# Float64 weights split ahead of their units and parked in DRAM

## The chip, the cores and the metric

One core of one Trainium2 chip runs the kernel. The metric is device time in microseconds (us) of one execution. Five engines work side by side, each through its own instructions in the order in which they were written: TensorE (PE), VectorE (DVE), ScalarE (ACT), GpSimd (POOL), and SyncE (SP), which issues nearly all DMAs.

## The reference

```python
# attention: state = w*state + k v^T per head, y = r (state + u k v^T)
x = attn_out.transpose(0, 2, 1, 3).reshape(B * S, H * D)       # 1536 x 384, float32
# layer 1: four experts of width 1024
p = domain_probs / (domain_probs.sum(-1, keepdims=True) + 1e-09)
for e in range(4):
    h = np.maximum(x @ w1[e], 0.0)
    out += p[:, e:e + 1] * (h @ w2[e])
# layer 2: width 2048, elu
h = x @ w_in
g = np.where(h > 0.0, h, alpha * (np.exp(np.minimum(h, 0.0)) - 1.0))
return (g @ w_out).astype(np.float32)
```

`w_in` and `w_out` of layer 2 are float64 arrays; all other inputs are float32.

## The kernel before

The attention runs in chunks of 128 tokens. Both layers run as six **units** of 1024 hidden columns: units 0 to 3 are the four experts, units 4 and 5 the two halves of the second layer. A unit goes over the 1536 tokens in blocks of 512 (unit 0, beside the attention, in blocks of 256), and a block has eight **steps** f = 0 to 7 of 128 hidden columns. A step issues a first-layer product `st1` (9 matmuls, line 610, into a bank `ph`), evacuates it (`evac`), and then issues the second-layer product `st2` (9 matmuls, line 646, into the three banks `po0` to `po2`) of an earlier step: two steps back in units 0 to 3, three steps back in units 4 and 5.

Every product is made of float32r parts: a weight `wh` (high) and `wl` (low), and an activation `hh` and `hl`. In units 0 to 3 ACT writes `hh` (line 622) and DVE `hl` (line 623). In units 4 and 5 `evac` is a longer chain: ACT writes `m` twice (lines 629, 630), DVE `g` (632), ACT `hh` (634), POOL `hl` (635). At the end of a block `po` is emptied: in units 1 to 3 by DVE into `t` (666), which POOL adds to `acc` (667), and after unit 3 ACT and POOL write from `acc` the new input of layer 2, `xh` (672) and `xl` (673); in unit 4 ACT copies `po` to `acc` (684).

A unit's weights are eight **slices** of 128 x 768 values: four of the first product, `(u, 1, i)`, and four of the second, `(u, 2, i)`. `split` (lines 493 to 538) turns a slice into `wh` and `wl` in one of 14 slots in SBUF (8, and NX = 6 once the attention's room is free). A float32 slice takes one copy on ACT and one subtraction on DVE. A float64 slice is read as two 32-bit words and takes eight DVE instructions (lines 519 to 534), a copy on ACT (529) and an addition on POOL (535), in four **stages** of two DVE instructions, with a yield behind each. `work` (540) is called behind every step but f = 1 and 2 and runs stages until its budget is spent; a stage "costs" 1.3 to 1.7, the budget is 0.9 up to unit 2 and 1.6 from unit 3 on:

```python
                    if not u or not BA <= f <= BB:
                        self.work(0.9 if u < NE - 1 else 1.6)
```

A slot is given back by `done` when the last block's product that reads it has been issued; the next `split` takes it. Slices are loaded by SP into three `raw` buffers (lines 482, 484). The order on every engine is that of the Python calls; nothing reorders it later.

Of the kernel before, what the change touches and what calls it, by code (L numbers as in the profile page):

```python
# [22 lines left out]
P = 128  # L23
B, H, S, D = 2, 8, 768, 48
NP = H // 2          # head pairs; a pair sits on partitions 0-47 and 64-111
NCB = S // P         # 128-token chunks of a batch row
NCH = B * NCB
N = B * S            # tokens
DM = H * D
KD = DM // P  # L30
NE, FF = 4, 1024     # experts, their width
NU = NE + 2          # the second layer's 2048 columns count as two more units
NF = FF // P
NX = 6               # slots for weights in the attention's room
WARM = 12            # products of zeros ahead of the first
NS = (2, 1, 2, 1, 1, 1, 1, 1)    # the attention's steps by step of the layers' first block
BA, BB = 1, 2        # the steps of a block that no weights are split in
TB = 512             # tokens of a block
# [8 lines left out]
# the upper words of float64s, read as float32s: of the largest and the least normal float32  # L47
# [3 lines left out]
class Fast:  # L51
    """Attention in chunks of 128 tokens, decays as w^t and w^-(s+1), which
    needs W_LO <= w <= W_HI (elsewhere w is held there, and the general path is taken).

    Rows of a pair of heads: 64 j + (index in the head). The chunk's part of a head's output,
    with its index on the rows, is v^T A + S^T r, where A[s, t] is (k_s w^-(s+1)).(r_t w^t)
    for s < t and r.u.k for s = t."""
# [27 lines left out]
    def bank(self):  # L85
        """The next bank: of three, and of the two layers' while those wait for the first x."""
        pool, tag = self.banks[self.nbank % len(self.banks)]
        self.nbank += 1
        return pool.tile([P, 512], F32, tag=tag, name=tag)

    def warm(self, n):
        """Products of zeros: the array's clock is halved while it has little to do."""
        nc = self.g.nc
        if self.zero is None:
            self.zero = self.c.tile([P, 512], BF16, name="zero")
            nc.vector.memset(self.zero, 0.0)
        pz = self.g.php.tile([P, 512], F32, tag="ph1", name="ph1")
        for _ in range(n):
            nc.tensor.matmul(pz, self.zero[:, 0:P], self.zero, start=True, stop=True)

    # r, k with their index on the rows
# [9 lines left out]
    # r, k, or v, with the tokens on the rows  # L111
# [49 lines left out]
    def setup_masks(self):  # L161
        nc = self.g.nc
        # 1 where t > s
        mf = self.c.tile([P, P], F32, name="mf")
        nc.gpsimd.memset(mf, 0.0)
        nc.gpsimd.affine_select(
            out=mf, in_=mf, compare_op=ALU.is_ge, fill=1.0, base=0,
            pattern=[[-1, P]], channel_multiplier=1)
        nc.gpsimd.tensor_copy(self.mask, mf)
# [25 lines left out]
    # r or k, scaled  # L195
# [9 lines left out]
    # the keys decayed to the chunk's end  # L205
# [6 lines left out]
    # r.u.k, by entries  # L212
# [8 lines left out]
    # the diagonal  # L221
    def s1d(self, ci):
# [3 lines left out]
        if ci < 2:  # L226
            # the first chunks' diagonal goes by itself
            self.va[ci] = va = self.p2.tile([P, DM], F32, tag="va", name="va")
            nc.vector.tensor_tensor(
                out=va.rearrange("t (h d) -> t h d", h=H), in0=self.v[ci].rearrange("t (h d) -> t h d", h=H),  # L230
                in1=a0.rearrange("s (h o) -> s h o", o=1).to_broadcast([P, H, D]), op=ALU.mult)
            return
# [10 lines left out]
    def s2(self, ci):  # L243
        nc = self.g.nc
        st = self.st[ci]
        # a bank for each of the two places of a head in its pair
# [13 lines left out]
    # the state's change, and the state  # L260
    def s3u(self, ci):
# [5 lines left out]
        # side by side, a head of a pair in each half of the array's columns  # L267
# [30 lines left out]
    def s3(self, ci):  # L298
# [5 lines left out]
        for p in range(NP):  # L304
# [4 lines left out]
            for j in range(2):  # L309
                # at first, all rows up to the second head's are to be written  # L310
                h, m = 2 * p + j, D if c or j else 64
                nc.tensor.matmul(  # L312
                    py[64 * j:64 * j + m, p, :], v[:, h * D:h * D + m], A[:, j, p, :],
                    start=not c, stop=True)
# [5 lines left out]
        if o:  # L320
            # the rows of all heads together, by way of DRAM
# [8 lines left out]
    # the first chunks': the rows of all heads together at once, v and S between zeros  # L330
# [5 lines left out]
    def s3f(self, ci):  # L336
# [3 lines left out]
        for kk in range(KD):  # L340
            # side by side, 64 rows of x in each half of the array's columns
# [22 lines left out]
class General:  # L364
    """Attention for any w: each state entry's recurrence is scanned along the tokens, with
    the key's index on the partitions and one column of the state at a time."""
# [8 lines left out]
    def run(self, ident, xT):  # L375
# [5 lines left out]
        # sel[:, e]: from row e, 64 + e to the rows of their halves; one: from the rows of a  # L381
        # half, with the window that starts at 64 - e, to row e, 64 + e
# [69 lines left out]
class Gen:  # L452
# [22 lines left out]
    def load_next(self):  # L475
        if self.nraw < len(self.slices):
            s = self.slices[self.nraw]
            u, kind, i = s
            t = self.wp.tile([P, 1536], I32, tag="raw", name="raw", bufs=self.NRAW)
            if u < NE:  # L480
                t = t[:, 0:768].bitcast(F32)
                self.nc.sync.dma_start(out=t, in_=self.ws[u, i, kind - 1])
            else:
                self.nc.sync.dma_start(out=t, in_=self.ws2[u - NE, i, kind - 1])
            self.raw[s] = t
            self.nraw += 1

# [5 lines left out]
    def split(self):  # L493
        """The next slice's two parts, in steps; each yields the time it takes of DVE."""
# [4 lines left out]
        pool, k = self.free.pop(0)  # L499
        self.slot[s] = (pool, k)  # L500
        hi = pool.tile([P, 768], F32R, tag=f"wh{k}", name=f"wh{k}")
        lo = pool.tile([P, 768], F32R, tag=f"wl{k}", name=f"wl{k}")
        if s[0] < NE:
            nc.scalar.copy(hi, t)  # L504
            self.weng.tensor_tensor(out=lo, in0=t, in1=hi.bitcast(F32), op=ALU.subtract)  # L505
            self.load_next()
            self.w_s[s] = (self.shape(hi, s[1]), self.shape(lo, s[1]))
            yield 0.9
            return
        # a float64 as two words: a = sign, exponent and the upper 20 fraction bits as a  # L510
        # float32 (0 below its normal range, its largest above), c = the 32 bits below
# [6 lines left out]
        v = nc.vector  # L518
        v.tensor_scalar(out=hf, in0=hf, scalar1=F64_MAX, scalar2=-F64_MAX, op0=ALU.min, op1=ALU.max)  # L519
# [16 lines left out]
        self.load_next()  # L536
        self.w_s[s] = (self.shape(hi, s[1]), self.shape(lo, s[1]))
        yield 1.7

    def work(self, budget):  # L540
        """Splits ahead, as far as there are slots, for about so much time of DVE."""
        while budget > 0:
            if self.cur is None:
                if not self.free or self.nspl == len(self.slices):
                    return
                self.cur = self.split()
# [20 lines left out]
    def probs(self, dp):  # L567
# [7 lines left out]
        # by expert, then tokens  # L575
# [41 lines left out]
    def evac(self, u, n, ph):  # L617
# [8 lines left out]
        else:  # L626
# [4 lines left out]
            # exp(min(h, 0)) - 1 is 0 where h > 0, and at least h elsewhere  # L631
# [57 lines left out]
    def count(self, c):  # L689
        """How many of w's entries the fast attention holds for."""  # L690
# [13 lines left out]
    def setup(self, ctx):  # L704
# [11 lines left out]
        self.free, self.slot, self.cur, self.weng = [], {}, None, self.nc.vector  # L716
        self.add_slots(self.wp, 8)
        # slices in the order of their splits: (unit, layer, slice)
        self.slices = [(u, kind, i) for u in range(NU) for i in range(4) for kind in (1, 2)]
        self.ident = self.cp.tile([P, P], F32, name="ident")  # L720

    def setup2(self, ctx):
        """What the attention's room is for once it is over."""
# [7 lines left out]
        self.sp = ctx.enter_context(tc.tile_pool(name="sp", bufs=1))  # L731

    def layers(self, tb0, before):
        """Both layers, the first unit in blocks of tb0 tokens. before(u, t0, f) is called
        ahead of a step and gives what is to come after its first product, if anything."""
        pend = []
        for u in range(NU):
            n = TB if u else tb0
            for t0 in range(0, N, n):
                for f in range(NF):  # L740
# [3 lines left out]
                    # the end of a block frees its banks before anything else  # L744
# [8 lines left out]
                    if not u or not BA <= f <= BB:  # L753
                        self.work(0.9 if u < NE - 1 else 1.6)
# [5 lines left out]
    def fast(self):  # L760
        tc, nc = self.tc, self.nc
        with ExitStack() as ctx:
# [21 lines left out]
            # attention; the first two chunks before the layers start  # L784
# [30 lines left out]
            self.work(0.1)   # w1, slice 0  # L815
# [7 lines left out]
            self.work(0.1)   # w2, slice 0  # L823
# [24 lines left out]
            for i in range(2, NCH):  # L848
                steps += [(f, c) for f, c in ((a1, i), (a2, i + 1), (a3, i)) if c < NCH]
                if i % 2 == 0 and i > 2:  # L850
                    # two steps after the last a3 of a pair
# [62 lines left out]
def laid_out(r, k, v, w, u, moe_domain_probs, moe_w1, moe_w2, moe2_w_in, moe2_w_out):  # L914
    def heads(a):       # head entries to rows 64 j + d of the pairs, 0 between
# [5 lines left out]
    # by chunk: rows 64 j + d, then r or k, pair, token; and rows of tokens, then r, k, v, entry  # L921
# [11 lines left out]
    # slices of 256 hidden columns: unit, slice, layer, row, then 768 values  # L933
# [31 lines left out]
```

## Time and profile before

| | |
|---|---|
| runs (3) | median 686.3 us, 685.81 to 689.27 |
| profiled execution, its span | 685.3 us; no other time of that execution is given, the median lies 1.0 us above it |
| TensorE busy | 666.9 us, 97% of the span |
| DVE, ACT, POOL busy | 352.6, 211.5, 208.0 us |
| mean granted TensorE clock | 0.984 |
| DMA | 48.11 MB, mean 70 GB/s |

A profile row is read as "line, engine, operation, out<-in". A name such as `wh` or `po` stands for all tiles of that name, and line numbers are those of the kernel before. "Idle before" is the time in which the engine stood still ahead of an instruction, with what released it. The clock is a share of 2.4 GHz: 1.00 is that level and 0.50 is 1.2 GHz.

### The profile page before, as it was taken

To read this page: it belongs to the slowest core of one execution; us is meant where nothing else is said; L and a number is where in the kernel's file an instruction comes from. 1 tells how busy PE (TensorE), PEld (TensorE's weight loads), DVE (VectorE), ACT (ScalarE), POOL (GpSimd) and SP (SyncE) were. 2 spreads that over 40 slices of the span, in tenths; PEclk is the share of its full clock that TensorE was granted. 3 is DMA by queue.
4 is the path that set the end of the run, shared out by engine and by line. 5 is a ranking of instruction groups with operands and counts; after the bars stand their busy time and mean duration, and the time that the engine had idled before them with its cause. 6 is when DMAs were issued, how large, how long until landed. Compare 5 with 4: busy or idle time off the path is not lost.

```text
span 685.3 us, 9098 instructions
## 1 busy us (share of the span) xinstructions
PE 666.9 (97%) x3701; PEld 557.4 (81%) x3701; DVE 352.6 (51%) x505; ACT 211.5 (31%) x358; POOL 208.0 (30%) x163
## 2 busy tenths in 40 slices
PE   8999999999999999999999999999997999999996
PEld 5788988899888888888888887888875888888884
DVE  7896566324544133422135696569596848212121
ACT  3232221123332113211122123133535454644441
POOL 5564563210002020202021225243744534333331
PEclk7899999999999999999999999999998999999999
DMA  8775542102421003210010221202121100001011
GB/s 256 216 215 165 171 148 69 34 15 70 162 92 47 0 3 107 99 47 0 1 55 38 93 92 47 92 7 88 46 92 46 47 0 1 0 1 47 0 47 52
DMA packets 18661, 48.11 MB, mean 70 GB/s; under 512 B 2145, under 2 KB 7698, under 8 KB 18610
## 3 DMA queue, kind: packets, MB, share of 16 engines
q1 hardware_dynamic: 18464, 47.42, 21.4%
q8 instruction: 31, 0.51, 0.3%
q14 instruction: 20, 0.16, 0.1%
q10 hardware_dynamic: 146, 0.03, 0.0%
HBM read 43.09 MB, written 4.35 MB: 69 GB/s over the span
## 4 chain that ended last, share of the span: by engine, by line
PE 84%; DVE 9%; issue 3%; POOL 2%; ACT 1%; DMA 0%; DVEq 0%; POOLq 0%; ACTq 0%
PE po L646 38%; PE ph L610 37%; PE pa L251 2%; PE pa L306 2%; PE pa L312 2%; DVE raw L519 1%; POOL acc L667 1%; DVE q L530 1%; DVE a L523 1%; DVE g L632 1%; DVE q L520 1%; DVE a L534 1%; DVE hl L623 1%; DVE a L527 1%; POOL wl L535 1%
## 5 line engine op out<-in xcount | busy, mean ns | idle before, releaser
L646 PE MATMUL po<-hh,wh 128*128 128x512 f32 (+1 forms) x504 | 183.4, 364 | 4.9 <-ACT acc L684 4.6
L646 PE MATMUL po<-hl,wh 128*128 128x512 f32 (+1 forms) x504 | 181.9, 361 | 1.9 <-POOL hl L635 1.7
L646 PE MATMUL po<-hh,wl 128*128 128x512 f32 (+1 forms) x504 | 181.5, 360 | 0.0
L610 PE MATMUL ph<-xh,wh 128*128 128x512 f32 (+1 forms) x504 | 177.7, 361 | 0.1
L610 PE MATMUL ph<-xh,wl 128*128 128x512 f32 (+1 forms) x504 | 177.1, 360 | 0.0
L623 DVE SCALAR_TENSOR_TENSOR hl<-ph,hh 128x512 fp32r<-128x512 f32 (+1 forms) x120 | 69.6, 582 | 179.9 <-ACT hh L622 179.2
L622 ACT ACTIVATE hh<-ph 128x512 fp32r<-128x512 f32 (+1 forms) x120 | 61.2, 512 | 281.9 <-PE ph L610 281.9
L610 PE MATMUL ph<-xl,wh 128*128 128x512 f32 (+1 forms) x504 | 126.1, 359 | 0.0
L646 PEld LDWEIGHTS po<-hh,wh 128*128 128x128 f32 x504 | 95.4, 189 | 22.4 <-ACT acc L684 5.0
L646 PEld LDWEIGHTS po<-hl,wh 128*128 128x128 f32 x504 | 95.6, 190 | 17.7 <-POOL hl L635 2.9
L610 PEld LDWEIGHTS ph<-xh,wh 128*128 128x128 f32 x504 | 95.5, 190 | 14.9 <-issue 0.4
L610 PEld LDWEIGHTS ph<-xh,wl 128*128 128x128 f32 x504 | 95.5, 189 | 14.1
L646 PEld LDWEIGHTS po<-hh,wl 128*128 128x128 f32 x504 | 95.5, 190 | 14.0
L610 PEld LDWEIGHTS ph<-xl,wh 128*128 128x128 f32 x504 | 88.3, 189 | 14.1
L635 POOL TENSOR_TENSOR hl<-g,hh 128x512 fp32r<-128x512 f32 x48 | 63.8, 1329 | 100.2 <-ACT hh L634 92.0
L667 POOL TENSOR_TENSOR acc<-acc,t 128x512 f32<-128x512 f32 x27 | 34.1, 1293 | 195.4 <-DVE t L666 195.4
L632 DVE SCALAR_TENSOR_TENSOR g<-m,ph 128x512 f32<-128x512 f32 x48 | 32.9, 684 | 92.0 <-ACT m L630 87.8
L535 POOL TENSOR_TENSOR wl<-a,raw 128x768 fp32r<-128x768 f32 x16 | 29.9, 1868 | 99.2 <-DVE a L534 59.2
L634 ACT CAST hh<-g 128x512 fp32r<-128x512 f32 x48 | 29.8, 622 | 68.0 <-DVE g L632 68.0
L629 ACT ACTIVATE m<-ph 128x512 f32<-128x512 f32 x48 | 28.6, 596 | 28.4 <-PE ph L610 28.2
L505 DVE TENSOR_TENSOR wl<-raw,wh 128x768 fp32r<-128x768 f32 x32 | 33.0, 1032 | 2.3 <-ACT wh L504 1.7
L233 POOL TENSOR_TENSOR A<-ident,a 128x1024 f32<-128x1024 f32 x10 | 20.7, 2071 | 43.5 <-DVE a L225 25.2
(103 smaller groups left out, 513.1 us busy)
## 6 DMA issues: line engine op xcount, KB each, us to landing
raw<-in_ws_dram SPq DMA_DIRECT2D x32, 384.0 KB, 3.0
raw<-in_ws_dram SPq DMA_DIRECT2D x16, 768.0 KB, 4.1
rk<-in_rkv_dram SPq DMA_DIRECT2D x12, 384.0 KB, 5.6
rkT<-in_rkT_dram SPq DMA_DIRECT2D x10, 448.0 KB, 5.2
pb<-pd SPq DMA_DIRECT2D x4, 768.0 KB, 3.9
v<-in_rkv_dram SPq DMA_DIRECT2D x12, 192.0 KB, 6.2
out_dram<-acc SPq DMA_DIRECT2D x9, 256.0 KB, 2.1
xd<-yT SPq DMA_DIRECT2D x10, 192.0 KB, 2.7
```

What stands on the lines that cost most here:

```text
L233: nc.gpsimd.tensor_tensor(out=self.A[ci % 2].rearrange("s j p t -> s p j t"), in0=self.g.ident.rearrange("s (a b t) -> s a b t", a=1, b=1) ...
L505: self.weng.tensor_tensor(out=lo, in0=t, in1=hi.bitcast(F32), op=ALU.subtract)
L535: nc.gpsimd.tensor_tensor(out=lo, in0=af, in1=cf, op=ALU.add)
L610: nc.tensor.matmul(ph[:, 0:n], a[:, kk, c0:c0 + P], b[:, kk], start=q == 0, stop=q == 3 * KD - 1)
L622: nc.scalar.activation(hh[:, 0:n], ph[:, 0:n], AF.Relu)
L623: nc.vector.scalar_tensor_tensor(out=hl[:, 0:n], in0=ph[:, 0:n], scalar=0.0, in1=hh[:, 0:n].bitcast(F32), op0=ALU.max, op1=ALU.subtract)
L629: nc.scalar.activation(m, ph, AF.Relu, scale=-1.0)
L632: nc.vector.scalar_tensor_tensor(out=gg, in0=m, scalar=-1.0, in1=ph, op0=ALU.add, op1=ALU.max)
L634: nc.scalar.copy(hh, gg)
L635: nc.gpsimd.tensor_tensor(out=hl, in0=gg, in1=hh.bitcast(F32), op=ALU.subtract)
L646: nc.tensor.matmul(po[:, 0:n], a[:, ff, i * P:(i + 1) * P], b[:, 0:n], start=f == 0 and q == 0, stop=f == NF - 1 and q == 2)
L667: nc.gpsimd.tensor_tensor(out=a, in0=a, in1=t[:, 0:n], op=ALU.add)
```

## The change

The float64 slices leave `split`. A new generator `narrow` runs the same ten instructions on them from unit 1 on, whenever no float32 slice has a free slot, into one pair of buffers `nh`, `nl`, instead of into a slot. `store` writes the pair to DRAM when the next `narrow` begins; `fetch` loads a stored pair by two DMAs into a slot when one is free and all float32 splits are done. The raw float64 words have two buffers `wide` of their own. NX goes from 6 to 4 (12 slots in all). The budget is 0.9 in unit 0 and 1.2 after.

```diff
-NX = 6               # slots for weights in the attention's room
+NX = 4
...
+    def load_wide(self):
+        if self.nwide < len(self.wide):
+            u, kind, i = self.wide[self.nwide]
+            t = self.sp.tile([P, 1536], I32, tag="wide", name="wide", bufs=2)
+            self.nc.sync.dma_start(out=t, in_=self.ws2[u - NE, i, kind - 1])
+            self.wraw.append(t)
+            self.nwide += 1
...
+    def store(self):
+        if self.made:
+            s, *parts = self.made.pop()
+            self.w_d[s] = d = self.dr.tile([2, P, 768], F32, name=f"w{s[0]}{s[1]}{s[2]}")
+            for i, t in enumerate(parts):
+                self.nc.sync.dma_start(out=d[i], in_=t.bitcast(F32))
+
+    def fetch(self):
+        while self.free and self.nget < len(self.wide) and self.wide[self.nget] in self.w_d:
+            s = self.wide[self.nget]
+            self.nget += 1
+            for i, t in enumerate(self.parts(s)):
+                self.nc.sync.dma_start(out=t.bitcast(F32), in_=self.w_d[s][i])
+
+    def narrow(self):
+        s = self.wide[self.nnar]
+        self.nnar += 1
+        t = self.wraw.pop(0)
+        hi = self.sp.tile([P, 768], F32R, tag="nh", name="nh")
+        lo = self.sp.tile([P, 768], F32R, tag="nl", name="nl")
...
+        self.store()
         v.tensor_scalar(out=hf, in0=hf, scalar1=F64_MAX, scalar2=-F64_MAX, op0=ALU.min, op1=ALU.max)
...
         nc.gpsimd.tensor_tensor(out=lo, in0=af, in1=cf, op=ALU.add)
-        self.load_next()
-        self.w_s[s] = (self.shape(hi, s[1]), self.shape(lo, s[1]))
+        self.made.append((s, hi, lo))
+        self.load_wide()
         yield 1.7
...
             if self.cur is None:
-                if not self.free or self.nspl == len(self.slices):
+                if self.nspl == len(self.slices):
+                    self.fetch()
+                if self.free and self.nspl < len(self.slices):
+                    self.cur = self.split()
+                elif self.sp and self.nnar < len(self.wide):
+                    self.cur = self.narrow()
+                else:
+                    self.store()
                     return
-                self.cur = self.split()
...
-                        self.work(0.9 if u < NE - 1 else 1.6)
+                        self.work(0.9 if not u else 1.2)
```

**DVE at the last steps of unit 3.** Before (`hl` is written once a step; `raw` is a float64 slice, `q` and `a` are scratch):

```order
L623 SCALAR_TENSOR_TENSOR hl_4055<-ph2_4044,hh_4054 128x512
L519 TENSOR_SCALAR raw_3806<-raw_3806 128x768
L520 TENSOR_SCALAR q_4069<-raw_3806 128x768
L523 SCALAR_TENSOR_TENSOR a_4070<-raw_3806,q_4069 128x768
L525 TENSOR_SCALAR q_4069<-raw_3806 128x768
L623 SCALAR_TENSOR_TENSOR hl_4086<-ph3_4075,hh_4085 128x512
L527 SCALAR_TENSOR_TENSOR a_4070<-q_4069,a_4070 128x768
L530 TENSOR_SCALAR q_4069<-a_4070 128x768
L532 SCALAR_TENSOR_TENSOR raw_3806<-raw_3806,q_4069 128x768
L534 TENSOR_TENSOR a_4070<-a_4070,wh11_4067 128x768
```

The same place after the change:

```order
L662 SCALAR_TENSOR_TENSOR hl_4163<-ph2_4152,hh_4162 128x512
L552 TENSOR_SCALAR wide_3973<-wide_3973 128x768
L553 TENSOR_SCALAR q_4197<-wide_3973 128x768
L662 SCALAR_TENSOR_TENSOR hl_4215<-ph3_4204,hh_4214 128x512
L556 SCALAR_TENSOR_TENSOR a_4198<-wide_3973,q_4197 128x768
L558 TENSOR_SCALAR q_4197<-wide_3973 128x768
L662 SCALAR_TENSOR_TENSOR hl_4240<-ph4_4229,hh_4239 128x512
L560 SCALAR_TENSOR_TENSOR a_4198<-q_4197,a_4198 128x768
```

Before, two stages (four instructions) stand between one `hl` and the next; now one stage (two instructions).

**SP over the end of unit 3.** Before, only loads of float64 slices stand there:

```order
L484 DMA raw_3806<-in_ws2_dram 128x1536
L484 DMA raw_3868<-in_ws2_dram 128x1536
L484 DMA raw_4042<-in_ws2_dram 128x1536
L484 DMA raw_4104<-in_ws2_dram 128x1536
L484 DMA raw_4162<-in_ws2_dram 128x1536
```

After (`wh11` and so on are slots, `w412` is the stored pair of slice (4, 1, 2)):

```order
L489 DMA wide_4150<-in_ws2_dram 128x1536
L532 DMA wh11_4175<-w412_3183 128x768
L532 DMA wl11_4176<-w412_3183 128x768
L532 DMA wh2_4179<-w422_3294 128x768
L532 DMA wl2_4180<-w422_3294 128x768
L532 DMA wh1_4183<-w413_3539 128x768
L532 DMA wl1_4184<-w413_3539 128x768
L532 DMA wh3_4187<-w423_3714 128x768
L532 DMA wl3_4188<-w423_3714 128x768
L532 DMA wh4_4191<-w510_3891 128x768
L532 DMA wl4_4192<-w510_3891 128x768
L524 DMA w511_4199<-nh_3998 128x768
```

Ten loads of stored pairs now stand between the load of a float64 slice and the store of the pair (`nh`, `nl`) of slice (5, 1, 1).

**ACT over the change from unit 3 to unit 4.** Before (`hh` of unit 3's last two steps, then unit 4's first `m`):

```order
L622 ACTIVATE hh_4085<-ph3_4075 128x512
L529 CAST wh11_4067<-a_4070 128x768
L622 ACTIVATE hh_4116<-ph4_4106 128x512
L629 ACTIVATE m_4149<-ph0_4137 128x512
L630 ACTIVATE m_4149<-m_4149 128x512
L634 CAST hh_4147<-g_4150 128x512
L529 CAST wh12_4129<-a_4132 128x768
L629 ACTIVATE m_4176<-ph1_4164 128x512
L630 ACTIVATE m_4176<-m_4176 128x512
```

After:

```order
L661 ACTIVATE hh_4214<-ph3_4204 128x512
L661 ACTIVATE hh_4239<-ph4_4229 128x512
L562 CAST nh_4195<-a_4198 128x768
L668 ACTIVATE m_4267<-ph0_4255 128x512
L669 ACTIVATE m_4267<-m_4267 128x512
L673 CAST hh_4265<-g_4268 128x512
L668 ACTIVATE m_4291<-ph1_4279 128x512
L669 ACTIVATE m_4291<-m_4291 128x512
L673 CAST hh_4289<-g_4292 128x512
```

Before, one copy of a slice stands behind unit 4's first `hh` and writes a slot (`wh12`). Now it stands ahead of unit 4's first `m`, and writes `nh`, which the store above reads.

## Rows read from the trace of the kernel before

**Rows 1.** Chain that ended last: shares of the span by engine.

```profile
PE 84%; DVE 9%; issue 3%; POOL 2%; ACT 1%; DMA 0%; DVEq 0%; POOLq 0%; ACTq 0%
```

**Rows 2.** Waits of TensorE: engine, line, releaser: us in total, times, longest.

```profile
PE po L646 <- ACT acc L684: 4.6, 1, 4.6
PE po L646 <- POOL hl L635: 1.7, 2, 1.4
```

**Rows 3.** Timeline, TensorE: start us, us, engine, line, out<-in, [idle before].

```profile
512.15 0.50 PE L646 MATMUL po<-hl,wh 128*128 128x512 f32 x1 [1.40 <-POOL hl L635]
...
520.90 0.80 PE L646 MATMUL po<-hh,wh 128*128 128x512 f32 x1 [4.56 <-ACT acc L684]
...
527.64 0.39 PE L646 MATMUL po<-hh,wh 128*128 128x512 f32 x1
```

**Rows 4.** Windows: us, busy (x) of PE PEld DVE ACT POOL, clock, DMA share, GB/s.

```profile
455.00:470.00 15.00, 15.00 (x68) 12.43 (x67) 14.31 (x17) 3.70 (x6) 3.73 (x2) 1.00 0.16 53
...
512.00:514.00 2.00, 1.85 (x8) 1.53 (x9) 1.86 (x3) 0.00 (x0) 0.10 (x1) 1.00 0.88 349
...
522.00:524.00 2.00, 2.00 (x6) 1.58 (x5) 0.69 (x1) 1.15 (x3) 0.26 (x1) 0.50 0.87 295
```

**Rows 5.** Chain that ended last, in order of time: start us, us, what.

```profile
531.89 2.04 PE po L646 x9
...
670.61 6.81 PE po L646 x30
```

**Rows 6.** Timeline, the change from unit 3 to unit 4.

```profile
468.70 0.39 PE L610 MATMUL ph<-xh,wh 128*128 128x512 f32 x1
...
477.94 1.88 DVE L666 TENSOR_TENSOR t<-po,pb 128x512 f32<-128x512 f32 x3
...
480.58 3.79 POOL L667 TENSOR_TENSOR acc<-acc,t 128x512 f32<-128x512 f32 x3
...
488.09 1.28 POOL L635 TENSOR_TENSOR hl<-g,hh 128x512 fp32r<-128x512 f32 x1
...
489.43 0.50 PE L646 MATMUL po<-hl,wh 128*128 128x512 f32 x1
```

**Rows 7.** Groups of instructions by shape: busy us, mean ns of one, idle before.

```profile
L622 ACT ACTIVATE hh<-ph 128x512 fp32r<-128x512 f32 x72 | 42.7, 598 | 198.0 <-PE ph L610 198.0
...
L623 DVE SCALAR_TENSOR_TENSOR hl<-ph,hh 128x512 fp32r<-128x512 f32 x72 | 49.4, 689 | 132.5 <-ACT hh L622 132.1
...
L535 POOL TENSOR_TENSOR wl<-a,raw 128x768 fp32r<-128x768 f32 x16 | 29.9, 1868 | 99.2 <-DVE a L534 59.2 <-issue 33.2 <-PE po L646 6.7
...
L532 DVE SCALAR_TENSOR_TENSOR raw<-raw,q 128x768 f32<-128x768 uint32 x16 | 15.3, 959 | 0.5
L534 DVE TENSOR_TENSOR a<-a,wh 128x768 f32<-128x768 f32 x16 | 15.2, 951 | 0.0
...
L529 ACT CAST wh<-a 128x768 fp32r<-128x768 f32 x16 | 13.4, 839 | 16.6 <-DVE a L527 16.6
```

**Rows 8.** DMA issues: out<-in, queue, count, KB each, median us to landing.

```profile
raw<-in_ws_dram SPq DMA_DIRECT2D x32, 384.0 KB, 3.0
raw<-in_ws_dram SPq DMA_DIRECT2D x16, 768.0 KB, 4.1
```

**Rows 9.** One line's instructions: landing time of the float32 loads, line 482.

```profile
DMA to landing us min/median/max: 2.8/3.0/7.6
```

**Rows 10.** Windows at the start, deep DMA queue; columns as in Rows 4.

```profile
10.00:12.00 2.00, 2.00 (x19) 2.00 (x19) 1.88 (x4) 0.51 (x1) 0.30 (x2) 0.50 1.05 416
...
18.00:20.00 2.00, 2.00 (x15) 1.27 (x13) 0.97 (x4) 1.05 (x3) 0.00 (x0) 0.50 1.06 260
```

**Rows 11.** Timeline, one undisturbed step of unit 5.

```profile
658.41 0.60 ACT L629 ACTIVATE m<-ph 128x512 f32<-128x512 f32 x1 [1.37 <-PE ph L610]
...
660.50 0.62 ACT L634 CAST hh<-g 128x512 fp32r<-128x512 f32 x1 [0.82 <-DVE g L632]
...
661.20 1.29 POOL L635 TENSOR_TENSOR hl<-g,hh 128x512 fp32r<-128x512 f32 x1 [2.79 <-ACT hh L634]
```

More of the change, by code (lines that the diff above doesn't have):

```diff
@@ L478, in load_next @@
             u, kind, i = s
[L479 to L484, printed above, removed]
+            t = self.wp.tile([P, 768], F32, tag="raw", name="raw", bufs=self.NRAW)
+            self.nc.sync.dma_start(out=t, in_=self.ws[u, i, kind - 1])
             self.raw[s] = t
             self.nraw += 1
+    def load_wide(self):
[5 more added lines that the diff above has]
+            self.nwide += 1
     def add_slots(self, pool, n):
@@ L498, in split, with parts @@
         t = self.raw.pop(s)
-        pool, k = self.free.pop(0)
-        self.slot[s] = (pool, k)
+        hi, lo = self.parts(s)
+        nc.scalar.copy(hi, t)
+        self.weng.tensor_tensor(out=lo, in0=t, in1=hi.bitcast(F32), op=ALU.subtract)
+        self.load_next()
+        yield 0.9
+    def parts(self, s):
+        self.slot[s] = pool, k = self.free.pop(0)
         hi = pool.tile([P, 768], F32R, tag=f"wh{k}", name=f"wh{k}")
         lo = pool.tile([P, 768], F32R, tag=f"wl{k}", name=f"wl{k}")
-        if s[0] < NE:
-            nc.scalar.copy(hi, t)
-            self.weng.tensor_tensor(out=lo, in0=t, in1=hi.bitcast(F32), op=ALU.subtract)
-            self.load_next()
-            self.w_s[s] = (self.shape(hi, s[1]), self.shape(lo, s[1]))
-            yield 0.9
-            return
+        self.w_s[s] = (self.shape(hi, s[1]), self.shape(lo, s[1]))
+        return hi, lo
+    def store(self):
[11 more added lines that the diff above has]
+    def narrow(self):
+        nc = self.nc
+        s = self.wide[self.nnar]
[3 more added lines that the diff above has]
+        lo = self.sp.tile([P, 768], F32R, tag="nl", name="nl")
         t = t.rearrange("p (n i) -> p n i", i=2)
@@ L535, in split @@
         nc.gpsimd.tensor_tensor(out=lo, in0=af, in1=cf, op=ALU.add)
-        self.load_next()
-        self.w_s[s] = (self.shape(hi, s[1]), self.shape(lo, s[1]))
+        self.made.append((s, hi, lo))
+        self.load_wide()
         yield 1.7
@@ L716, in setup @@
         self.free, self.slot, self.cur, self.weng = [], {}, None, self.nc.vector
+        self.sp, self.made, self.wraw, self.w_d = None, [], [], {}
+        self.nwide = self.nnar = self.nget = 0
         self.add_slots(self.wp, 8)
-        self.slices = [(u, kind, i) for u in range(NU) for i in range(4) for kind in (1, 2)]
+        self.slices, self.wide = (
+            [(u, kind, i) for u in us for i in range(4) for kind in (1, 2)]
+            for us in (range(NE), range(NE, NU)))
         self.ident = self.cp.tile([P, P], F32, name="ident")
@@ L731, in setup2 @@
         self.sp = ctx.enter_context(tc.tile_pool(name="sp", bufs=1))
+        self.load_wide()
+        self.load_wide()
     def layers(self, tb0, before):
```

## The prediction

> **What bounds the kernel now.** I read the chain that ended last first: 84% of the span on TensorE, 9% on DVE [rows 1]. So products set the time, except where DVE holds them up, and I looked for that place with the waits of TensorE [rows 2]: one wait of 4.6 us for ACT's copy out of `po`, and 1.7 us, of which one wait is 1.40 us [rows 3], for POOL's `hl`. All stand at 506 to 521 us, in the first block of unit 4. In an undisturbed stretch a half step of nine products takes 2.04 us [rows 5], a step 4.08.
>
> The waits have a tail. TensorE resumes at 520.90; the 18 products from there take until 527.64, 6.74 us instead of 4.08 [rows 3], since the granted clock is 0.50 (1.2 GHz) in 522 to 524 [rows 4]. That is 2.66 us lost. After the gap of 1.40 us the clock was still 1.00 (2.4 GHz) in 512 to 514 [rows 4].
>
> Sum: 4.56 + 1.70 + 2.66 = 8.9 us. Check: from the first product of unit 4 at 468.70 [rows 6] there are 48 first-layer and 50 second-layer half steps, 98 x 2.04 = 199.9, which would end at 668.6, with 0.2 of pipeline at 668.8; the last product ends at 670.61 + 6.81 = 677.42 [rows 5]. So 8.6 to 8.9 us; I take 8.8. Before unit 4 nothing in units 1 to 3 is lost: TensorE is busy in all of 455 to 470 although DVE is busy 14.31 of 15 us [rows 4].
>
> **The change part by part.**
>
> *Float64 splits at one stage a step.* Before, two stages stand behind each step from unit 3 on, so that DVE has no slack, and in unit 4 the longer chain from `m` to `hl` runs through DVE. Now one stage stands there, from unit 1 on. At the double rate TensorE lost nothing in unit 3 [rows 4], so the single rate in units 1 to 3 costs nothing; the idle time of DVE covers it, and without that cover a late `hl` would show, as in [rows 2]. In unit 4 one stage a step is left up to the third block. A stage of about 1.9 us (two of 0.95 us [rows 7]) and `g` fit in 4.08. The backlog goes, and with it the 8.8 us. What is late next?
>
> *Slots, loads, stores.* Two slots fewer only make float32 splits wait for free slots, and a unit needs eight of 12. Sixteen stores and sixteen loads of pairs, 64 DMAs of 384 KB, lie beside the products. The price is on SP's queue and in the one pair of buffers: a slice's copy on ACT into `nh` has to wait until the store of the previous pair has landed, and every later ACT instruction stands behind it. Usually there is room: from the load of `wide` to that copy are some 9 us, against 1.9 + 3 x 1.1 us for `wide` and the store. At the end of unit 3 ten loads stand in between.
>
> *That place, step by step.* Let t = 0 be the start of unit 3's step f = 5 in the last block, 456.46 in the trace (468.70 less six half steps). POOL finishes `nl` of slice (5, 1, 1), whose stage 4 stands in the step before: `ph` of that step is ready at -1.8, then 0.60 for `hh`, 0.69 for `hl`, 0.96 + 0.95 on DVE and 1.87 on POOL [rows 7], with small gaps 3.45. That frees the `wide` buffer, and SP issues the next `wide` load and behind it the ten loads of pairs; the slots they fill are free by 4.1. A load of 384 KB lands 3.0 us after its issue, one of 768 KB after 4.1 [rows 8]: 1.1 us more per 384 KB, and 1.9 fixed. In units of 384 KB the queue holds 2 (`wide`) + 10 + 1 (the store of `nh`) = 13, so the store lands at X = 3.45 + 1.9 + 13 x 1.1 = 19.65.
>
> That the store stands behind the loads shows in rows as the landing time of equal loads: 2.8 us at least, 7.6 at most where the queue was full [rows 9]. The Trainium skill, "DMA: Bandwidth & Descriptors", section "Queues, rings and completion order", says the same as a rule: descriptors on each DMA engine are consumed in ring order, and all of SP's DMAs share one row of rings. By that rule, which speaks against the change, the one store that ACT waits for cannot pass the ten loads, and the sum is the one below; if it could pass them, it would be rival 2's. The Trainium skill, same page, section "Anatomy of one DMA", fits 2.0 us + bytes / 436 GB/s for another issue path: 5.1 MB would give X = 17.2, an estimate, and a gap of 1.3 us, a total of 678.8. I keep the rows' 1.1 us.
>
> ACT reaches the copy at about 12.6 (`ph` of f = 7 at 10.4, `hh`, `hl`, one DVE instruction) and stands until X. From there:
> - `nh` 0.84 [rows 7]. Unit 4's first step: from `m` to the end of `hl` 4.08 us, to the end of ACT's `hh` 2.71 [rows 11], so `hl` ends at X + 4.95.
> - Second step: `m` starts at X + 3.56. DVE has stage 4 (1.91) between the two `g`, and ends the second `g` at X + 5.65. POOL has `nl` (1.87), then `hl`: X + 8.2.
> - DVE's `t`: 1.88 [rows 6], X + 5.65 to X + 7.55.
> - POOL: three `acc`, three `xl`, then the third step's `hl`. From the start of `acc` to the end of that `hl` was 489.37 - 480.58 = 8.79 [rows 6]. So X + 17.0.
>
> TensorE needs that `hl` at 489.43 - 0.10 in the old trace, t = 32.87 [rows 6]; there the wait was only 0.1 us, since `acc` began at t = 24.1. So the bound is X = 15.9, and the loss is X - 15.9 = 3.75 us. Part of it comes earlier: `po0` is free only at X + 6.3 = 26.0, needed at 24.5, a gap of about 1.4, and then one of 2.3. Behind it, POOL needs 1.3 us of each 4.08, so the lag is worked off; the next queue of loads (four, at the start of unit 4) ends before ACT needs it.
>
> Does the clock fall in a gap of 2.3 us? A gap of 1.40 left it, one of 4.56 did not. 2.3 is nearer to the first, so I take none; if it falls, 2.66 us more.
>
> Sum: -8.8 + 3.75 = -5.05. The profiled execution's span of 685.3 becomes 680.2; the median of the runs lies 1.0 above that span: 686.3 - 5.05 = 681.2.
>
> The unknown is the rate of a deep queue. At the start of the program it was 416 GB/s in 10 to 12 us and 260 in 18 to 20 [rows 10], 0.95 and 1.51 us per 384 KB. X is then 17.6 or 25.0, the gap 1.7 or 9.1. With the clock held: 679.2 at best; at worst 686.6, with the clock's 2.66 689.2. The landing times of whole loads of this very size are nearest, so 1.1 stands.
>
> **Rivals.**
> 1. *The gap is there and the clock falls in it.* For: the gap of 4.56 us did it. Against: the one of 1.40 didn't. 686.3 - 8.8 + 3.75 + 2.66 = 683.9.
> 2. *No gap.* The store lands before 15.9, because the ten loads don't run one behind the other as I add them, or ACT does not wait for them. Then all is gained: 677.5. Against: the queue's 14.3 us would have to be 3.75 us, a quarter, shorter.
> 3. *Slower.* The ten loads are 3 KB rows, read while stores write; at the rate of 18 to 20 us the store lands at 25.0, ACT stands from 12.6 on, and 9.1 + 2.66 us are lost for 8.8 won: 689.2. It decides from X = 22.0 on, where gap and clock together eat 8.8: 1.28 us per 384 KB, 306 GB/s. For: 260 GB/s was seen. Against: 349 GB/s in 512 to 514 [rows 4], a single load.
> 4. *It doesn't do what it says.* Part of unit 5's slices is still split in unit 4's first two blocks, where the old waits were; if `g` is late there with one stage too, the wait for ACT's copy out of `po` stays: 4.56 + 2.66 us are not won, and with the new gap 686.3 - 1.7 + 3.75 = 688.4. Against: half the DVE work per step.
>
> **How the numbers follow.** My forecast (gap, clock held) 0.45; rival 1 0.22; rival 2 0.15; rival 3 0.10; rival 4 0.08. Predicted: 681.2. The range of the forecast alone is 679 to 683.5. The range for 8 in 10 reaches over rivals 1 and 2 and into the near part of 3 and 4: 677.0 to 688.0. Half a per cent, 3.4 us, is what a measurement can tell from no change. Faster by more: the forecast but for its far end, rival 2, and a little of rival 1 with a small gap: 0.57. Slower by over 0.5%, above 689.7: the far ends of rivals 3 and 4: 0.08. The rest 0.35.
>
> **What would show it.** The wait for `acc` at the first change of block in unit 4 is gone, and the clock is 1.00 there. In place of it ACT's copy into `nh` at the change from unit 3 to 4 waits for a DMA, some 7 us long; the store lands 16 us after the `wide` load's issue; TensorE waits in two pieces, for DVE's `t` and for POOL's `hl`, 3 to 4 us in all. No wait of TensorE in units 1 to 3. Wrong would be: no DMA wait of ACT (rival 2), over 6 us of it on TensorE (rival 3), a wait in units 1 to 3, or the old wait in unit 4.

## The result, and the profile after

The changed kernel takes 681.5 us (median of 4 runs, 680.9 to 682.8) against 687.2 us for the kernel before in runs on the same chips; the ratio is 0.9913, 95% interval 0.9890 to 0.9935. The same kernel in later runs (run 5 below) gave 0.9911 (0.9891 to 0.9932). The forecast of 681.2 us, faster, came true. The profiled execution took 682.0 us with a span of 680.2, the span that the sum gave. That it fits so closely is luck in part: two of the sum's terms were too small by 2 us each, and their errors cancelled; the runs below show which.

The chain that ended last in the changed kernel, shares of the span by engine and then by line:

```profile
PE 92%; DMA 3%; POOL 1%; DVE 1%; ACT 1%; SPq 1%; issue 0%; ACTq 0%; POOLq 0%
```

TensorE's share rose from 84 to 92% [rows 1], DVE's 9% went to 1%, and DMA stands in the chain. The waits of TensorE, by line and releaser (us in total, times, longest), answer to [rows 2]:

```profile
PE po L685 <- ACT hh L673: 2.1, 2, 1.5
PE po L685 <- POOL hl L674: 1.2, 1, 1.2
```

The 4.6 us for ACT's copy out of `po` are gone. The new ones stand at the change from unit 3 to 4, as TensorE's timeline there shows (start, us, engine, line, out<-in, idle before):

```profile
467.71 0.39 PE L649 MATMUL ph<-xh,wh 128*128 128x512 f32 x1
...
481.61 0.47 PE L685 MATMUL po<-hh,wh 128*128 128x512 f32 x1 [1.50 <-ACT hh L673]
...
490.60 0.50 PE L685 MATMUL po<-hh,wh 128*128 128x512 f32 x1 [0.57 <-ACT hh L673]
492.30 0.50 PE L685 MATMUL po<-hl,wh 128*128 128x512 f32 x1 [1.21 <-POOL hl L674]
...
673.13 0.39 PE L685 MATMUL po<-hh,wl 128*128 128x512 f32 x1
```

Behind the last of them the granted clock falls to 0.50 (1.2 GHz) and is back at 2.4 GHz by 497, and where the old wait stood it is 1.00 throughout (windows; columns as in [rows 4]):

```profile
490.00:492.00 2.00, 0.52 (x2) 0.19 (x1) 0.19 (x1) 1.67 (x3) 2.00 (x2) 1.00 1.00 395
492.00:494.00 2.00, 1.70 (x6) 1.37 (x7) 1.53 (x3) 1.44 (x3) 1.02 (x2) 0.81 0.45 180
494.00:496.00 2.00, 2.00 (x7) 1.52 (x6) 1.56 (x3) 1.18 (x3) 0.88 (x2) 0.50 0.00 0
496.00:498.00 2.00, 2.00 (x9) 1.64 (x8) 2.00 (x2) 0.88 (x2) 1.11 (x1) 0.84 0.00 0
...
500.00:550.00 50.00, 50.00 (x222) 41.42 (x221) 33.34 (x31) 27.11 (x45) 21.82 (x16) 1.00 0.30 95
```

What makes them late is one instruction of ACT, the copy into `nh` (ACT's timeline, then its waits by releaser):

```profile
465.93 0.60 ACT L661 ACTIVATE hh<-ph 128x512 fp32r<-128x512 f32 x1 [3.48 <-PE ph L649]
474.74 0.84 ACT L562 CAST nh<-a 128x768 fp32r<-128x768 f32 x1 [8.22 <-DMA w<-nh]
475.49 0.59 ACT L668 ACTIVATE m<-ph 128x512 f32<-128x512 f32 x1
...
ACT nh L562 <- DVE a L560: 19.2, 15, 2.0
ACT nh L562 <- DMA w<-nh: 8.2, 1, 8.2
```

Fifteen of the sixteen copies wait for DVE alone; this one waits for the store of the previous pair. SP's issues show where that store stood (SPq is SP's sequencer):

```profile
458.73 0.33 SPq L489 DMA_DIRECT2D wide<-in_ws_dram  x1
459.16 0.39 SPq L532 DMA_DIRECT2D wh<-w  x1
...
465.25 0.32 SPq L532 DMA_DIRECT2D wl<-w  x1
466.19 0.32 SPq L524 DMA_DIRECT2D w<-nh  x1
```

The ten loads go out between 459.16 and 465.25, the store behind them at 466.19, and it lands just before ACT goes on at 474.74, 16.0 us after the issue of `wide`: 7.5 us until it is issued and 8.5 on the way.

**A measure without the start.** Of equal executions some reach the end of unit 0's 256-token products 1 to 2 us later than others, from waits in the attention's part that the change does not touch and, in the four latest of the table, half clock there (0.50 from 31.9 to 38.7 us in the second profile of after). So I count from the first product behind the last of them, which is at one place of TensorE's order in all kernels, to the last product. In the run with the store ahead of the loads (below) TensorE is busy from end to end between the two: 182.08 to 667.40 (the starts of those two products), 485.32 us. What a kernel takes above that is lost:

| execution | from | to | us | lost |
|---|---|---|---|---|
| before | 181.94 | 678.38 | 496.44 | 11.12 |
| after | 182.08 | 673.13 | 491.05 | 5.73 |
| after, second profile | 183.87 | 672.96 | 489.09 | 3.77 |
| before, single rate in two blocks | 183.06 | 671.76 | 488.70 | 3.38 |
| store ahead of the loads | 182.08 | 667.40 | 485.32 | 0 |
| store in the last stage | 183.75 | 669.07 | 485.32 | 0 |
| three pairs at a time | 183.99 | 669.92 | 485.93 | 0.61 |
| products in the gap | 183.64 | 672.67 | 489.03 | 3.71 |
| late, double rate | 182.06 | 685.14 | 503.08 | 17.76 |

11.12 - 5.73 = 5.4 us won between the two profiled executions; the spans differ by 5.1. The row of the products in the gap holds 2.04 us of those nine products themselves.

### The profile page after: what moved, and what is told of

The parts are those of the page before. It is cut to its first block, busy times and chain, and to the rows that moved or that the text cites. A ratio compares the mean times of both kernels' runs of the same rounds, so it can differ in the third digit from the quotient of the medians.

```text
span 680.2 us, 9215 instructions
## 1 busy us (share of the span) xinstructions
PE 665.5 (98%) x3701; PEld 556.3 (82%) x3701; DVE 339.8 (50%) x505; ACT 213.2 (31%) x358; POOL 206.4 (30%) x163
## 4 chain that ended last, share of the span: by engine, by line
PE 92%; DMA 3%; POOL 1%; DVE 1%; ACT 1%; SPq 1%; issue 0%; ACTq 0%; POOLq 0%
PE po L685 42%; PE ph L649 42%; PE pa L306 2%; PE pa L312 2%; PE pa L251 2%; DMA w<-nh 1%; DMA v<-in_rkv_dram 1%; DMA wh<-w 1%; PE pa L353 1%; POOL acc L706 1%; PE pa L272 1%; PE ph L354 0%; POOL xl L712 0%; PE ph L353 0%; DVE acc L725 0%
## 5 line engine op out<-in xcount | busy, mean ns | idle before, releaser
L568 POOL TENSOR_TENSOR nl<-a,wide 128x768 fp32r<-128x768 f32 x16 | 29.9, 1869 | 190.4 <-DVE a L567 157.7
L506 DVE TENSOR_TENSOR wl<-raw,wh 128x768 fp32r<-128x768 f32 x32 | 31.5, 998 | 5.0 <-ACT wh L505 4.6
```

The lines of the kernel that those rows point to most:

```text
L568: nc.gpsimd.tensor_tensor(out=lo, in0=af, in1=cf, op=ALU.add)
```

## Experiments

Ratios are to the kernel before on the same chip.

**1. Was it the second stage behind a step?** In the kernel before:

```
-                        self.work(0.9 if u < NE - 1 else 1.6)
+                        self.work(0.9 if u < NE - 1 or u == NE and t0 < 2 * TB else 1.6)
```

> The kernel before with one change: in the first two blocks of unit 4 one split stage stands behind a step instead of two. Theory: TensorE's waits at the start of unit 4's second block (1.70 us for POOL's hl, 4.56 us for ACT's copy out of po, then 2.66 us at half clock) come from the second stage on DVE, so all three go: 686.3 - 8.8 = 677.5 us, span near 676.5, ratio 0.987; the short gaps in unit 3 near 416 us (0.33 and 0.23 us) stay, since the double rate stays there. Rival: the wait for the copy out of po has to do with the order on ACT and POOL at the end of a block, not with the splits: it stays at 4 to 5 us and the time within 1 us of 686. Second rival: the splits left over are late for unit 5, with a new wait there and less than half of the gain.

Measured: 681.8 us (679.4 to 685.9), ratio 0.9916 (0.9891 to 0.9940). At the place of [rows 3] TensorE is busy in all 20 us with the clock at 1.00 (windows, columns as in [rows 4]):

```profile
510.00:520.00 10.00, 10.00 (x46) 8.29 (x45) 3.67 (x5) 6.85 (x12) 3.84 (x3) 1.00 0.14 55
520.00:530.00 10.00, 10.00 (x46) 8.29 (x45) 8.48 (x9) 5.43 (x9) 4.57 (x5) 1.00 0.00 0
```

But a shorter wait of the same kind stands at the change from unit 4 to unit 5, behind unit 4's third block, to which the double rate is left here:

```profile
582.09 0.50 PE L646 MATMUL po<-hh,wh 128*128 128x512 f32 x1 [1.93 <-ACT acc L684]
```

Of the 9.99 us lost in unit 4 none is left, and 2.2 are new behind its end. The theory holds, and the wait follows the second stage: the ratio of 0.987 that I expected left out that it would come back there. The first rival is refuted: the wait for the copy out of `po` in unit 4 goes without any change to the order at the end of a block. The second is refuted as I put it: all three waits of TensorE in the counted stretch are for ACT or DVE, none for late weights, and 5.6 us of the 8.8 are won (687.4 - 681.8).

**2. The store ahead of the loads.** In the kernel after:

```
                 if self.nspl == len(self.slices):
-                    self.fetch()
+                    n = len(self.w_d)
+                    self.store()
+                    self.fetch(n)
...
-        while self.free and self.nget < len(self.wide) and self.wide[self.nget] in self.w_d:
+        while self.free and self.nget < n:
```

> The kernel after, with the store of a finished pair issued ahead of the loads of the pairs that find a free slot, not behind them. Theory: ACT's wait of 8.2 us at the change from unit 3 to 4 is the store's place in SP's queue. With the store behind the wide load alone it lands about 3.45 + 1.9 + 3 x 1.1 = 8.65 us after the start of that step, ACT reaches the copy at 11.0, so the wait is 0, both gaps of TensorE (1.66 and 2.2 us) and the half clock behind them (1.75 us) go: span 680.2 - 5.7 = 674.5, 676 us in all, ratio to before 0.984. Rival: the order does not matter, since the DMA engines serve loads and stores side by side and the store is slow by itself (its median landing is 6 us): ACT still waits over 4 us, TensorE over 2, span 678 or more.

Measured: 677.7 us (676.4 to 680.1), ratio 0.9871 (0.9835 to 0.9906), span of the profile 674.5. SP's issues and ACT's copy:

```profile
458.71 0.33 SPq L489 DMA_DIRECT2D wide<-in_ws_dram  x1
459.13 0.38 SPq L524 DMA_DIRECT2D w<-nh  x1
...
460.08 0.97 SPq L532 DMA_DIRECT2D wh<-w  x1
...
467.82 0.32 SPq L532 DMA_DIRECT2D wl<-w  x1
```

```profile
468.19 0.84 ACT L562 CAST nh<-a 128x768 fp32r<-128x768 f32 x1 [1.67 <-DVE a L560]
```

Nothing but the order on SP differs, and ACT waits only for DVE: the copy stands at 468.19 and not at 474.74, so the store's place cost ACT 6.55 us. TensorE does not wait from unit 1 to the end (window; columns as in [rows 4]):

```profile
182.00:667.00 485.00, 485.00 (x2143) 401.60 (x2142) 225.99 (x298) 164.36 (x263) 138.03 (x100) 1.00 0.28 95
```

This is the rule weighed in the prediction (the Trainium skill, "DMA: Bandwidth & Descriptors", section "Queues, rings and completion order"): descriptors are consumed in ring order. The trace agrees as far as the 8.5 us go that after's store took behind what was in flight (the last load lands at 473.7, the store at 474.6), against 2.3 us for the quickest store of that kernel; the 7.5 us ahead of its issue are SP's own order. The same store, moved so that `wide` alone stands ahead of it, took 6.0 us here and was in time. The stores' line in the kernel after:

```profile
DMA to landing us min/median/max: 2.3/6.1/8.6
```

**3. Three pairs at a time**, the store still behind them:

```
     def fetch(self):
-        while self.free and ...
+        n = self.nget + 3
+        while self.nget < n and self.free and ...
```

> The kernel after, with at most three pairs (six loads) taken at a time, not all that find a slot; the store stays behind them. Theory: the queue ahead of the store is 2 + 6 + 1 units of 384 KB instead of 13, X = 3.45 + 1.9 + 9 x 1.1 = 15.25 us, so ACT still waits about 4 us at its copy, but TensorE's bound was X = 15.9 (15.4 by the gaps measured): no gap of TensorE over 0.3 us there, clock 1.00, span about 674.5, ratio 0.984. Rival: a wait of ACT is passed on to TensorE in proportion: half of the wait leaves half of the gaps, 1.9 us and part of the half clock, span 677 to 678. Second rival: the loads that were put off are late or form a second queue in unit 4, with a new wait of ACT there.

Measured: 679.0 us (678.4 to 679.5), ratio 0.9878 (0.9847 to 0.9909). ACT and TensorE:

```profile
473.11 0.84 ACT L563 CAST nh<-a 128x768 fp32r<-128x768 f32 x1 [4.67 <-DMA w<-nh]
```

```profile
490.72 0.50 PE L686 MATMUL po<-hl,wh 128*128 128x512 f32 x1 [0.32 <-POOL hl L675]
```

This execution runs 1.91 us behind after's from the start on, so the copy stands 15.73 us after the start of unit 3's step f = 5 (15.25 expected, 19.27 with ten loads). ACT's wait went from 8.2 to 4.7 us, TensorE's loss from 5.73 (4.08 without the half clock) to 0.61: not in proportion. There is a slack up to about X = 15, and only what goes beyond it is paid. The span of 677.1 was above the 674.5 that I expected, 1.9 us of it from the start and 0.6 from this gap.

**4. Products in the gap**, nine of them ahead of the second-layer products of unit 4's f = 2:

```
+                    if first and first[0] == NE and first[1] == 0 and first[3] == 2:
+                        self.fill(9)
                     if first:
                         self.st2(*first)
```

> The kernel after, with nine products (128x512, into a bank that nobody reads) put ahead of the second-layer products of unit 4's step f = 2, where TensorE stood 0.74 and 1.47 us; nothing else is moved, and the result is not touched. Theory: the clock of 1.2 GHz from 493.2 to 496.7 us follows from TensorE standing still there; with the products in the gap it stays at 2.4 GHz, and the 1.75 us lost at half clock go while the wait for hl stays as it is, covered by the products: span 680.2 - 1.75 = 678.4. Rival: the clock falls all the same, set off by the first gap at 480 us or by something else: span 680.2 with half clock near 493 to 497. Second rival: the nine products are themselves in the way (they need 2.04 us, the gap had 2.2): up to 0.5 us more.

Measured: 681.0 us (680.1 to 682.9), ratio 0.9910 (0.9874 to 0.9946). The clock stays up behind the filled gap:

```profile
490.00:494.00 4.00, 3.94 (x18) 2.96 (x17) 1.78 (x3) 2.32 (x5) 3.41 (x3) 1.00 0.95 366
494.00:496.00 2.00, 2.00 (x10) 1.63 (x9) 1.12 (x3) 1.38 (x3) 1.48 (x1) 1.00 0.06 25
```

That would fit the theory, were it not for run 5: there the clock stayed up without the products. The experiment settles nothing. Its span was 679.7, not the 678.4 that I expected.

**5. The kernel after once more**, as the measure for runs 6 and 7.

> The kernel after once more, beside the next two on the same chip, as their measure. Theory: 11.1 us of waiting and half clock behind unit 1 are gone and 5.7 us are new at the change from unit 3 to 4; ratio to before 0.991 to 0.993, ACT's copy waits 7.5 to 8.5 us for the store. Rival: the earlier 5.7 us were a matter of one execution; ratio under 0.987 and the wait under 4 us.

Measured: 681.8 us (681.1 to 683.0), ratio 0.9911 (0.9891 to 0.9932). ACT waited 7.9 us for the store, TensorE's gaps were 1.18, 0.54 and 1.21 us, and the clock did not fall:

```profile
490.00:494.00 4.00, 2.25 (x9) 1.35 (x8) 1.42 (x3) 2.32 (x5) 3.72 (x4) 1.00 0.98 359
494.00:496.00 2.00, 2.00 (x10) 1.64 (x10) 1.11 (x3) 1.75 (x3) 1.30 (x1) 1.00 0.19 75
```

```profile
483.07 0.47 PE L685 MATMUL po<-hh,wh 128*128 128x512 f32 x1 [1.18 <-ACT hh L673]
492.06 0.50 PE L685 MATMUL po<-hh,wh 128*128 128x512 f32 x1 [0.54 <-ACT hh L673]
493.78 0.50 PE L685 MATMUL po<-hl,wh 128*128 128x512 f32 x1 [1.21 <-POOL hl L674]
```

So the mechanism repeats, the 5.7 us do not quite: 3.77 are lost here, and its span of 680.1 holds 1.8 us from a later start.

**6. The store in the last stage**, the shortest form of run 2:

```
         self.made.append((s, hi, lo))
+        self.store()
         self.load_wide()
```

> The kernel after, with the store issued at the end of a pair's last split stage, ahead of the next wide load and of all loads of pairs (one line added). Theory: as with the store ahead of the loads alone, ACT waits for no store and TensorE for nothing behind unit 1: span near 674.5, ratio 0.983 to 0.987, 4 to 6 us under the kernel after in the same call. Rival: SP now stands at the store until POOL has written nl, with the wide load and float32 loads queued behind it, so that splits in units 1 and 2 come late: a wait of TensorE or of ACT there, ratio over 0.989.

Measured: 676.9 us (675.4 to 677.9), ratio 0.9838 (0.9814 to 0.9862): 4.9 us under after in the runs beside it, and faster than both kernels. Nothing is lost in the counted stretch, so the rival (SP held up at the store, splits late) did not happen.

**7. The old time and rate of the splits, with the new way through DRAM**, from the kernel of run 2 with the line of run 6:

```
-                elif self.sp and self.nnar < len(self.wide):
+                elif self.late and self.nnar < len(self.wide):
...
+                    self.late = u >= NE - 1
...
-                        self.work(0.9 if not u else 1.2)
+                        self.work(0.9 if u < NE - 1 else 1.6)
```

> The kernel with the store ahead of the loads (and at the end of the last stage), but the time and rate of the float64 splits as before: none in units 1 and 2, two stages behind a step from unit 3 on, so that 28 stages fall into unit 4. The way of the pairs through DRAM stays. Theory: the waits of before come from the second stage behind a step, not from where the pairs are kept: 1.1 us at the start of unit 3 and 8 to 10 us at the start of unit 4's second or third block come back (wait for ACT's copy out of po, then half clock), span 683 to 686. Rival: the old wait had to do with writing straight into the slots or with loads of raw weights, and is gone with the new way: span 674.5 to 677. Second rival: two stages behind a step leave the store too little time, and ACT waits for it in unit 3.

Measured: 694.6 us (694.2 to 697.9), ratio 1.0113 (1.0082 to 1.0144). The old wait is back, twice, by the waits of TensorE, and behind the shorter one the clock falls too (window; columns as in [rows 4]):

```profile
PE po L688 <- ACT acc L726: 8.6, 2, 5.5
PE po L688 <- POOL hl L677: 2.2, 4, 1.5
```

```profile
563.00:565.00 2.00, 2.00 (x6) 1.51 (x6) 0.69 (x1) 1.18 (x3) 0.19 (x1) 0.50 0.00 0
```

The waits come from when and at what rate the splits run; the DRAM detour without the early start is slower than the kernel before. ACT waits for no store, so the second rival falls. The 17.76 us lost are more than the 9 to 11 that I expected, and the span of 692.3 lies above the 683 to 686; the second wait, 3.05 us and half clock behind it, was not in [rows 3]. Why it comes here and not in the kernel before was not tried.

## Why the prediction was right, and where its terms were off

| step of the prediction | forecast | measured |
|---|---|---|
| the stall in unit 4 that goes | 8.8 | 9.99 |
| lost in units 1 to 3 before | 0 | 1.13 |
| the store lands, X | 19.65 | 19.27 |
| ACT could copy at | 12.6 | 12.72 |
| TensorE's two gaps | 3.75 | 4.08 and 3.77 |
| half clock behind them | 0 | 1.65 and 0 |
| net | -5.05 | -5.39 by the table, -5.1 by the spans, -5.7 by the medians |

- *The old stall goes*: right, and for the reason given (runs 1 and 7). It stood in unit 4's second block (which begins near 501 us), not in its first, as the prediction has it. The size was 1.2 us short. I had checked the sum against an end at 677.42, a row of the chain [rows 5]; the last product starts at 678.38. From the first product of unit 4 to the last are 678.38 - 468.70 = 209.68 us before and 667.40 - 467.71 = 199.69 in run 2. What the idle times leave out: they count from the end of a product of 0.39 us, though the next would have started 0.23 us behind its start, and behind each gap the next product follows after 0.3 to 0.6 us, not 0.23.
- *"Before unit 4 nothing in units 1 to 3 is lost"*: wrong. I read the window of 455 to 470 us, at the end of unit 3. In that unit's second block two gaps, with their restarts, cost 1.1 us under the double rate, and the changed kernel, at the single rate, has none. They stood among the waits that I passed over. The timeline of the kernel before, with the last product of all:

```profile
417.07 0.49 PE L646 MATMUL po<-hh,wh 128*128 128x512 f32 x1 [0.33 <-ACT hh L622]
417.79 0.50 PE L646 MATMUL po<-hl,wh 128*128 128x512 f32 x1 [0.23 <-DVE hl L623]
...
678.38 0.39 PE L646 MATMUL po<-hh,wl 128*128 128x512 f32 x1
```

- *The store behind ten loads*: right in place, order and size. The wait was 8.2 us by the profile, which counts from the end of ACT's last instruction; against the copy of run 2 it is 6.55 (forecast 19.65 - 12.6 = 7.05). The rate of the deep queue, the unknown of the range, was 1.08 us per 384 KB ((16.0 - 1.9) / 13), beside the 1.1 taken from whole loads. The Trainium skill's fit ("DMA: Bandwidth & Descriptors", section "Anatomy of one DMA") had made X an estimated 17.2; the measurement is 2.1 us above it and decides.
- *Two gaps of 1.4 and 2.3*: 1.50, and 0.57 + 1.21 in two pieces. The first is put down to ACT's `hh`, which ends at 481.56; by the program `po0` waits for DVE's first `t`, which ends 0.05 us before it. The profile names only the release that came last. That the gaps come so near to 3.75 is luck too: the store landed earlier than forecast (X = 19.27 and, in the second profile, 18.96), but the chain from the copy to the third `hl` took 17.5 us (474.74 to 492.25), not 17.0. In it one subtraction on DVE took 2.06 us instead of 0.95 (last section), and POOL, busy without a break from there to the third `hl`, stood 0.95 us for it:

```profile
480.45 1.85 POOL L568 TENSOR_TENSOR nl<-a,wide 128x768 fp32r<-128x768 f32 x1 [0.95 <-DVE a L567]
```

- *Clock held*: wrong in the first execution, right in the second. Rival 1 happened at 1.65 of its 2.66 us. With the prediction's own gain that would have been 683.2 (686.3 - 8.8 + 5.73); that the time still came out at 681.5 is due to the 2.3 us by which the gain was too small, less the error of the base (next item). Rivals 2 to 4 did not happen; run 2, with the store moved, is what rival 2 described.
- *From the span to the time*: the 1.0 us mixed the span of one execution with the median of others. The executions for which both are on record take 1.75 to 1.94 us more than their span (the profiled one 682.0 against 680.2). So the profiled execution before took some 687.1 us (an estimate from its span of 685.3), and with a fourth run the kernel before has a median of 687.2, 0.9 above the 686.3 that the forecast starts from. From there the forecast's -5.05 would have given 682.1.

Open stays what decides whether the clock falls behind these gaps. From unit 1 on it held after gaps of 1.40 and 1.93 us, fell in or behind gaps of 3.05, 4.56 and 5.51, fell behind the group of 1.50, 0.57 and 1.21 us and held after that of 1.18, 0.54 and 1.21.

## What to carry to other kernels

A store that frees a buffer is on the path of whoever fills that buffer next: issue it ahead of loads that nobody needs soon, as one added line gave 4.9 us here, beside 5.7 for the whole change. Read a wait's cost at the bound engine as what exceeds the slack, not as its length (4.7 us cost 0.6; 7.9 cost 3.8, and 8.2 cost 4.1 and the half clock). And when a stall is priced from a trace, count from a fixed product to the last product, since idle times leave out the restarts and the end of a chain row is not the end of the work.

## What the hardware showed that I had not expected

The burst's issues come at two paces. The first loads go out 0.43 us apart (459.16, 459.59), the last 0.94 to 1.27 us apart (463.98, 465.25, 466.19). In the program each of SP's DMAs takes the next of eight semaphores and waits until that one's last DMA has landed, so about eight are in flight, and from there on SP goes at the pace of the landings: the store at 466.19 goes out just behind the landing of the third load, eight places ahead of it, at 466.1. That is why the store was issued 7.5 us after `wide`, and why its own landing time shows only half of what it waited.

The subtraction on DVE just behind the copy took 2.06 us, 16 of its kind 0.95 in the median:

```profile
478.25 2.06 DVE L567 TENSOR_TENSOR a<-a,nh 128x768 f32<-128x768 f32 x1
478.20 1.30 POOL L674 TENSOR_TENSOR hl<-g,hh 128x512 fp32r<-128x512 f32 x1 [19.50 <-ACT hh L673]
...
L567 DVE TENSOR_TENSOR a<-a,nh x16: 951/953/2064, 206.9 to 566.2; 128x768 f32<-128x768 f32 x16
```

The sixteen fall into two kinds. Eleven ran while POOL did nothing and took 0.95 us; five, all in unit 4, began just after the start of POOL's `hl` and took 2.05 to 2.06. The other kernels here agree: 2.05 to 2.07 us wherever the subtraction begins beside `hl`, 0.95 elsewhere, and in the kernel before, where none of the sixteen meets work of POOL, all take 0.95. So the longer time goes with POOL's work beside it; why was not tried. The prediction had this stage at 1.91 us, from rows of the kernel before.
